# Attention, gated convolution and spatial gating on one core: block moves by DMA, convolution taps over batch borders, and another order in the first tile

## The chip, the cores and the metric

The kernel runs on one core of a Trainium2 chip. The metric is the device time of one execution in microseconds (us), median of several runs. TensorE (PE) has a clock gate with two levels, 1.2 and 2.4 GHz; the granted clock in the profile is the share of the full one.

## What is computed

Eight batches of 576 tokens. First an attention within chunks of 64 tokens (8 heads of 64), then a gated feed-forward layer with a convolution over three tokens, then a second layer with a spatial mix; all in float32. The change lies in the first two:

```
scores = scale * (q_c @ k_c.T)                    # per chunk of 64 tokens
scores = scores - max(scores)
attn = exp(scores) / (sum(exp(scores)) + 1e-9)
x = attn @ v_c
h = maximum(x @ w_in, 0)
conv = cw[0]*h[t-1] + cw[1]*h[t] + cw[2]*h[t+1]   # zero beyond a batch's first and last token
gate = 1 / (1 + exp(-conv))
y = (h * gate) @ w_out
```

The convolution doesn't cross from one batch into the next: the first token of a batch has no left neighbour, the last no right one. The 4608 tokens are laid in one row, so that a batch border falls inside a tile of tokens.

## The kernel before

Phase A makes attention and the first layer, phase B the second layer. Phase A goes over ten tiles (`TILES`: eight of 512 tokens, two of 256); a tile has `KF` = 8 slots, one for each 128 rows of `w_in`'s output. Slot s = 8 * tile + f. In each slot, `moe_in(s)` makes 12 matmuls into a PSUM tile `h` (three products of high and low halves, L467), `moe_h(s)` the ReLU (L487, ScalarE, ACT) and the convolution: the middle tap `c = h * cw[1]` (L492 on GpSimd, POOL, in slots below `START` = 9, else L494 on ACT), then the outer taps on VectorE (DVE, L500). A tap writes only columns that have their neighbour in the same batch, so where a border lies in a tile each outer tap is two instructions (`runs` gives the pieces), and a slot has four. `moe_tanh(s - 1)` (L509, ACT), `moe_g(s - 1)` (L513, DVE) and `moe_split(s - 2)` (high and low half, ACT L521 and DVE L79 `gl`) follow in later slots, and `moe_out` sums the slot into four PSUM tiles `acc` (L546): of slot s-2 for the first tile, of slot s-3 afterwards. The first tile's `moe_out` uses the float32 weights `w2f`, 8 matmul records per slot.

Attention goes in 18 groups of 256 tokens, two to a 512 tile, each in two halves j. `att_s` makes scores (L255, PE) in PSUM `a0`/`a1`; `att_sm1` takes the maximum (L270 `mx`) and the difference (L276 `e`) on DVE, `att_exp` the exponential on ACT (L299, one instruction), `att_sm2` sum (L310), inverse and product (L319) on DVE. For halves listed in `ACC`, the subtraction and the sum go with eight exponentials on ACT (L294). The block P must be transposed for P @ V: groups below `NP` = 6 do it by PE (`att_tp`, L358 `tp`) and an ACT copy (L364); the later groups by DVE's transpose of 32x32 pieces (L328 `t`), after which 8 blocks of 32 partitions move into `pt`: four that stay in their partitions by POOL copies (L339), four by DMAs of SP's queue (L341). `att_pv` (L397 `px`, L416 `x`) multiplies by V into PSUM `a0`/`a1` again, and its result goes to `xh`, `xl`.

`FIRST_SLOTS`, `S_SLOT` and `PV_SLOT` say in which slot a group's scores and products stand: from tile 4 on, a tile's first group has its scores in slot 5 of the tile two before and its product in slot 1 of the tile before, the second group scores in slot 3 and product in slot 7, of the tile before. Halves j = 0, 1 go through the softmax in the slot of the scores and the next one. `start_slot` writes out slots 0 to 8, the loop behind it the others; every engine does its instructions in the order in which this code issues them. A prelude ahead of slot 0 does groups 0 and 1.

Of the kernel before, what the change touches and what calls it, by code (L numbers as in the profile page):

```python
# [7 lines left out]
F32 = mybir.dt.float32  # L8
# [33 lines left out]
LAG0 = 2  # L42
# [2 lines left out]
P0 = sum(g[0] == 0 for g in GROUPS)  # L45
NP = 6

ACC = ((0, 1), (2, 0), (2, 1), (3, 0), (3, 1))
RBUFS = 4

S_SLOT = (-3, 3)
PV_SLOT = (1, 7)

FIRST_SLOTS = {1: ((1, 5), (4, 8)), 2: ((1, 5), (3, 8)), 3: ((-1, 3), (1, 7))}

LATE_S = ()

FRONT = (0, 7)
NS = KF * NT
START = KF + 1  # L60
WMAX = 64 * max(TILES)

# [9 lines left out]
def attention_moe_kernel(ctx: ExitStack, tc: tile.TileContext, qT, kT, vL, vP, eye, w1, cw, w2, w3, wsp, wsr, bsp, w4, out):  # L72
# [103 lines left out]
    def phase_a(mid):  # L176
# [124 lines left out]
        def sm2_steps(g, j):  # L301
# [23 lines left out]
            def turn():  # L325

                t = ap.tile([128, 2, 8, 32], F32, tag="t", name="t", bufs=2)
                nc.vector.transpose(  # L328
                    out=t[:, :, :nu, :].rearrange("p h u j -> p u h j"),
                    in_=e.rearrange("p u (h i) -> p u h i", h=2),  # L330
                )
                pt = d["pt", j] = ap.tile([128, 2, 8, 32], F32, tag="pt", name="pt", bufs=4)
                for hh in range(2):
                    for qh in range(2):
                        for kh in range(2):
                            s0, o0 = 64 * hh + 32 * qh, 64 * hh + 32 * kh
                            dst, src = pt[o0:o0 + 32, qh, :nu, :], t[s0:s0 + 32, kh, :nu, :]
                            if qh == kh:
                                nc.gpsimd.tensor_copy(out=dst, in_=src)  # L339
                            else:  # L340
                                nc.sync.dma_start(out=dst, in_=src)  # L341

            return ([] if acc else [total]) + [eps, inverse, norm]

# [94 lines left out]

            return high, low  # L440

        hs, hhs, gs, accs = {}, {}, {}, {}

        carry = mp.tile([128, KF, 2], F32, name="carry", bufs=1)

# [34 lines left out]
        def moe_h(s, between=lambda: None):  # L480
# [7 lines left out]
            if i < NT - 1:  # L488
                nc.gpsimd.tensor_copy(out=carry[:, f, :], in_=h[:, w + b - 2:])
            c = mp.tile([128, WMAX], F32, tag="c", name="c", bufs=3)[:, :n]  # L490
            if s < START:
                nc.gpsimd.tensor_scalar_mul(c, h[:, o:o + n], cws[:, 1, f:f + 1])  # L492
            else:
                nc.scalar.activation(out=c, in_=h[:, o:o + n], func=AF.Copy, scale=cws[:, 1, f:f + 1])  # L494
            prev = runs(n, lambda j: o + j > 0 and (t0 + j) % S != 0)
            nxt = runs(n, lambda j: o + j + 1 < w + b and (t0 + j) % S != S - 1)
            between()
            for tap, step, segs in ((0, -1, prev), (2, 1, nxt)):
                for a, z in segs:
                    nc.vector.scalar_tensor_tensor(  # L500
                        out=c[:, a:z], in0=h[:, o + a + step:o + z + step], scalar=cws[:, tap, f:f + 1],
                        in1=c[:, a:z], op0=ALU.mult, op1=ALU.add,
                    )
            gs[s] = (h[:, o:o + n], c)

        def moe_tanh(s):
            _, c = gs[s]

            nc.scalar.activation(out=c, in_=c, func=AF.Tanh, scale=0.5)  # L509

# [136 lines left out]
        def scores(s):  # L647
            if s in at:
# [4 lines left out]
                for j in range(2):  # L653
                    if s < START:
                        todo.setdefault((s, 1), []).append((g, j))
                        todo[s + 1, 2 + j] = [(g, j)]
                        todo[s + 2, 4] = [(g, 1)]
                        if g < NP:
                            todo[s + 2, 5 + j] = [(g, j)]
# [12 lines left out]

        def start_slot(s):

            moe_hh(s)
            tps = [att_tp(*h) for h in todo.pop((s, 5), [])]
            if s < KF:
                moe_in(s)
            if s == KF:
                xh, xl = values(s)  # L680
            scores(s)
            if s:
                moe_tanh(s - 1)
                moe_g(s - 1)
            for f in tps:
                f()
            att_sm2(*todo.pop((s, 4), []))
            tps = [att_tp(*h) for h in todo.pop((s, 6), [])]
            first.load(2)
            if s == 4:  # L690
                load_v(3)
            weave(first.merge(2))
            soft = todo.pop((s, 2), [])
            for h in soft:
                att_exp(*h)
            att_sm2(*soft)
            if s == KF:
                xh()
                xl()
            if s >= LAG0:  # L700
                moe_out(s - LAG0)
            if s == KF:
                moe_in(s)
            moe_h(s)
            for f in tps:
                f()
            for h in todo.pop((s, 3), []):
                att_exp(*h)
            if first.merged:
                first.high()  # L710
                first.low()
            first.scale(2)
            if s < KF:
                xh, xl = values(s)
                xh()
                xl()
            att_sm1(*todo.pop((s, 1), []))

        def out(s):
            if s - LAG0 < KF:  # L720
# [4 lines left out]
        for s in range(NS + LAG):  # L725
# [17 lines left out]
                moe_hh(s)  # L743
            xs = ()
            tp = todo.pop((s, 7), None)
            if tp:
                tp = att_tp(*tp)
            if s % KF in FRONT:
                xs = values(s)
# [5 lines left out]
                moe_split(s - 2)  # L755
            if s < NS + 1:
                moe_tanh(s - 1)
            if tp:
# [338 lines left out]
```

## Time and profile before

| | before |
|---|---|
| median of 3 runs | 953.56 us (953.29 to 954.04) |
| profiled execution, device time | 949.09 us |
| its span in the trace | 947.0 us |
| mean granted TensorE clock | 0.982 |
| busy: PE, DVE, ACT, POOL | 906.8, 597.8, 419.7, 146.5 us (96, 63, 44, 15% of the span) |

The profiled execution is one run; what lies around its span is 2.1 us, and it is 4.5 us below the median. Phase A takes the span's first 523 us, phase B the rest. A busy share is a mean over stages that differ; where PE stands still is to be read from the order of time.

### The profile page before, as it was taken

Reading aid. Unit: us, or ns where it says so; the run is one execution under the profiler, and the core shown is the slowest. Engines: PE = TensorE matmul, PEld = TensorE weight load, DVE = VectorE, ACT = ScalarE, POOL = GpSimd, SP = SyncE. Lnnn points to the kernel's source line nnn. Section 1 sums busy time; section 2 is a strip of 40 time slices with the busy share of each in tenths; the row PEclk is TensorE's granted clock in tenths of the full one; section 3 lists DMA queues with packets and bytes.
Section 4 is the critical chain, followed back from the end, with each engine's and each line's share of the span. In section 5 each row is a group of like instructions: output and inputs, shape, how many; then the busy total and the mean of one; then the engine's idle time right before and its main releaser. Section 6 shows DMA issues by size and latency. Waiting matters only on the chain.

```text
span 947.0 us, 17151 instructions
## 1 busy us (share of the span) xinstructions
PE 906.8 (96%) x6804; PEld 769.8 (81%) x6804; DVE 597.8 (63%) x1173; ACT 419.7 (44%) x869; POOL 146.5 (15%) x305
## 2 busy tenths in 40 slices
PE   7699788999999999999999999999999999999998
PEld 6465567877777787778899898989898898989897
DVE  5775787998979798885767575451717162542522
ACT  4554453555564544546467454242423333332321
POOL 0221233232413233230311020010001000000000
PEclk8889999999999999999999999999999999999999
DMA  9551223434242341321023431112020302020001
GB/s 302 186 183 46 90 67 102 144 103 140 88 131 84 96 145 34 120 83 46 12 83 87 145 115 51 46 45 84 1 84 13 116 13 82 13 67 12 22 24 56
DMA packets 62352, 79.52 MB, mean 84 GB/s; under 512 B 6720, under 2 KB 49856, under 8 KB 62144
## 3 DMA queue, kind: packets, MB, share of 16 engines
q1 hardware_dynamic: 62272, 78.43, 26.1%
q8 instruction: 53, 0.87, 0.4%
q14 instruction: 27, 0.22, 0.1%
HBM read 54.29 MB, written 18.87 MB: 77 GB/s over the span
## 4 chain that ended last, share of the span: by engine, by line
PE 77%; DVE 10%; issue 4%; ACT 3%; DMA 2%; POOL 2%; SPq 1%; ACTq 0%; POOLq 0%
PE h L467 15%; PE acc L546 14%; PE pss L971 13%; PE psu L937 11%; PE pso L990 11%; PE psv L885 10%; DVE c L500 3%; PE x L416 1%; POOL c L492 1%; DVE gl L79 1%; DMA x2d<-x 1%; DVE mx L270 1%; DVE e L276 1%; DVE e L319 1%; PE s L255 1%
## 5 line engine op out<-in xcount | busy, mean ns | idle before, releaser
L500 DVE SCALAR_TENSOR_TENSOR c<-hh,nr,c 128x257 f32<-128x257 f32 (+28 forms) x272 | 134.9, 546 | 62.6 <-ACT c L494 43.7
L973 DVE TENSOR_TENSOR gf<-pss,bb 128x288 f32<-128x288 f32 x64 | 28.9, 452 | 146.5 <-PE pss L971 146.5
L509 ACT ACTIVATE c<-c 128x512 f32<-128x512 f32 (+2 forms) x80 | 47.5, 594 | 109.1 <-DVE c L500 109.1
L467 PE MATMUL h<-xh,w1h 128*128 128x512 f32 (+1 forms) x320 | 89.1, 402 | 1.0 <-DVE xh L434 0.9
L467 PE MATMUL h<-xh,w1l 128*128 128x512 f32 (+1 forms) x320 | 83.8, 385 | 0.0
L467 PE MATMUL h<-xl,w1h 128*128 128x512 f32 (+1 forms) x320 | 81.2, 376 | 0.0
L971 PE MATMUL pss<-wsh,vl 128*128 128x288 f32 x256 | 75.4, 295 | 0.0
L971 PE MATMUL pss<-wsh,vh 128*128 128x288 f32 x256 | 75.4, 294 | 0.0
L971 PE MATMUL pss<-wsl,vh 128*128 128x288 f32 x256 | 75.3, 294 | 0.0
L546 PE MATMUL acc<-gh,w2l 128*128 128x512 f32 (+2 forms) x288 | 71.5, 370 | 0.0
L546 PE MATMUL acc<-gl,w2h 128*128 128x512 f32 (+2 forms) x288 | 71.4, 370 | 0.0
L546 PE MATMUL acc<-gh,w2h 128*128 128x512 f32 (+2 forms) x288 | 71.2, 369 | 0.0
L467 PEld LDWEIGHTS h<-xh,w1l 128*128 128x128 f32 x320 | 59.4, 196 | 13.1 <-DVE w1l L79 0.4
L975 ACT CAST gth<-gf 128x288 fp32r<-128x288 f32 x64 | 27.7, 433 | 95.5 <-DVE gf L974 95.5
L339 POOL COPY pt<-t 32x256 f32<-32x256 f32 x96 | 49.7, 518 | 126.2 <-issue 60.0
L467 PEld LDWEIGHTS h<-xl,w1h 128*128 128x128 f32 x320 | 57.8, 191 | 12.2
L467 PEld LDWEIGHTS h<-xh,w1h 128*128 128x128 f32 x320 | 56.7, 196 | 13.6 <-issue 1.4
L487 ACT ACTIVATE hh<-h 128x512 f32<-128x512 f32 (+1 forms) x80 | 44.0, 550 | 37.9 <-PE h L467 37.8
L983 POOL CAST grh<-gth 128x256 fp32r<-128x256 f32 x8 | 5.3, 668 | 358.0 <-ACT gth L975 358.0
L79 DVE TENSOR_TENSOR gl<-c,gh 128x512 fp32r<-128x512 f32 (+2 forms) x72 | 52.6, 730 | 11.6 <-ACT gh L521 11.6
L546 PEld LDWEIGHTS acc<-gh,w2l 128*128 128x128 f32 x288 | 50.8, 188 | 10.2
L546 PEld LDWEIGHTS acc<-gl,w2h 128*128 128x128 f32 x288 | 50.8, 188 | 10.2
(126 smaller groups left out, 1910.5 us busy)
## 6 DMA issues: line engine op xcount, KB each, us to landing
raw<-in_w_dram SPq DMA_DIRECT2D x26, 512.0 KB, 4.9
x2f<-x2d SPq DMA_DIRECT2D x32, 288.0 KB, 3.1
q<-in_qT_dram SPq DMA_DIRECT2D x16, 512.0 KB, 3.9
k<-in_kT_dram SPq DMA_DIRECT2D x16, 512.0 KB, 4.9
out_dram<-o SPq DMA_DIRECT2D x32, 256.0 KB, 2.1
v<-in_vP_dram SPq DMA_DIRECT2D x6, 512.0 KB, 6.1
v<-in_vL_dram SPq DMA_DIRECT2D x12, 256.0 KB, 3.6
v<-in_vL_dram SPq DMA_DIRECT2D x24, 128.0 KB, 3.5
```

The costliest lines, as they stand in the source:

```text
L79: eng.tensor_tensor(out=lo, in0=full, in1=hi, op=ALU.subtract)
L339: nc.gpsimd.tensor_copy(out=dst, in_=src)
L467: nc.tensor.matmul(ph, wt[:, k, f * 128:(f + 1) * 128], x[:, k, :w], start=n == 0, stop=n == 11)
L487: nc.scalar.activation(out=h[:, b:], in_=ph, func=AF.Relu)
L500: nc.vector.scalar_tensor_tensor(out=c[:, a:z], in0=h[:, o + a + step:o + z + step], scalar=cws[:, tap, f:f + 1], in1=c[:, a:z], op0=ALU.m ...
L509: nc.scalar.activation(out=c, in_=c, func=AF.Tanh, scale=0.5)
L546: nc.tensor.matmul(accs[m], w[:, f, m * 128:(m + 1) * 128], x, start=f == 0 and j == 0, stop=f == KF - 1 and j == len(terms) - 1,)
L885: nc.tensor.matmul(ps, x[:, k, sl], w[:, k, DV:], start=i == 0, stop=i == 11)
L937: nc.tensor.matmul(ps[:, :HB], w[:, k, d * 128:(d + 1) * 128], x[:, k, t], start=i == 0, stop=i == 11)
L971: nc.tensor.matmul(o, a[:, ds], w, start=i == 0, stop=i == len(mm) - 1)
L973: nc.vector.tensor_tensor(out=gf, in0=o, in1=bb[:, t], op=ALU.add)
L990: nc.tensor.matmul(ps, x[:, k, sl], w[:, k, :], start=i == 0, stop=i == 11)
```

## The change

1. All eight blocks of a transposed half move by DMA from SP's queue (96 POOL copies become 96 more DMAs).
2. Outer taps are one instruction each, over the batch border. The two columns at the border that so get a wrong neighbour are made again by ACT: a product `m` of the middle tap (one column), and, ahead of `moe_tanh`, an activation that adds the one right neighbour to it. That is four ACT instructions of one column in each of 56 slots, and two DVE instructions fewer.
3. `ACC` keeps only (0, 1): the halves of groups 2 and 3 take the difference and the sum on DVE and one exponential on ACT.
4. In slots below `START` the middle tap is on ACT, not on POOL.
5. Slots 0 to 7 get an order written as a list (`ORDER`); slot 8 keeps its own (`LAST_ORDER`). PE's transposes move behind `moe_out`. In later slots, `TP_LATE` puts the transposes behind `moe_in`. The scores of group 5 move from slot 13 to slot 12, and the copies `xh` behind the exponential.

```diff
-ACC = ((0, 1), (2, 0), (2, 1), (3, 0), (3, 1))
+ACC = ((0, 1),)
-FIRST_SLOTS = {1: ((1, 5), (4, 8)), 2: ((1, 5), (3, 8)), 3: ((-1, 3), (1, 7))}
+FIRST_SLOTS = {1: ((1, 5), (4, 8)), 2: ((1, 4), (3, 8)), 3: ((-1, 3), (1, 7))}
+ORDER = "hh in s g norm1 load merge exp0 norm0 out tp0 h pt0 exp1 split scale tp1 pt1 pv x max"
+LAST_ORDER = "hh tp0 pv s g pt0 norm1 tp1 load merge exp0 norm0 x out in h pt1 exp1 split scale max"
+TP_LATE = True
@@ turn
-                            if qh == kh:
-                                nc.gpsimd.tensor_copy(out=dst, in_=src)
-                            else:
-                                nc.sync.dma_start(out=dst, in_=src)
+                            nc.sync.dma_start(out=dst, in_=src)
@@ moe_h
-            if s < START:
-                nc.gpsimd.tensor_scalar_mul(c, h[:, o:o + n], cws[:, 1, f:f + 1])
-            else:
-                nc.scalar.activation(out=c, in_=h[:, o:o + n], func=AF.Copy, scale=cws[:, 1, f:f + 1])
+            nc.scalar.activation(out=c, in_=h[:, o:o + n], func=AF.Copy, scale=cws[:, 1, f:f + 1])
-            for tap, step, segs in ((0, -1, prev), (2, 1, nxt)):
+            fixes[s] = []
+            for tap, step, segs, other in ((0, -1, prev, nxt), (2, 1, nxt, prev)):
+                if len(segs) == 2:
+                    (a, j), (_, z) = segs
+                    segs = [(a, z)]
+                    m = mp.tile([128, 1], F32, tag="m", name="m", bufs=8)
+                    nc.scalar.activation(out=m, in_=h[:, o + j:o + j + 1], func=AF.Copy, scale=cws[:, 1, f:f + 1])
+                    fixes[s].append((c[:, j:j + 1], h[:, o + j - step:o + j - step + 1], cws[:, 2 - tap, f:f + 1], m))
@@ moe_tanh
+            for dst, src, w, m in fixes.pop(s):
+                nc.scalar.activation(out=dst, in_=src, func=AF.Identity, scale=w, bias=m)
@@ the loop over slots from START on
-            if tp:
+            if tp and not TP_LATE:
                 tp = att_tp(*tp)
...
-            if xs:
-                xs[0]()
             if soft:
                 att_sm1(soft)
                 att_exp(*soft)
+            if xs:
+                xs[0]()
...
                 moe_in(s)
+                if tp and TP_LATE:
+                    tp = att_tp(*tp)
                 moe_h(s)
+                if tp and TP_LATE:
+                    tp()
```

**PE, slots 2 and 3.** `h` rows are `moe_in`, `acc` rows `moe_out`, `tp` rows the transposes of group 2's two halves. Before, from the `moe_out` of slot 2 to that of slot 3:

```order
L546 MATMUL acc_575<-c,w2f 128x512
L358 MATMUL tp<-idt,e 128x128 x4
L467 MATMUL h<-xh,w1h 128x512 x4
L467 MATMUL h<-xl,w1h 128x512 x4
L467 MATMUL h<-xh,w1l 128x512 x4
L358 MATMUL tp<-idt,e 128x128 x4
L546 MATMUL acc_572<-c,w2f 128x512
```

And now:

```order
L555 MATMUL acc_569<-c,w2f 128x512
L468 MATMUL h<-xh,w1h 128x512 x4
L468 MATMUL h<-xl,w1h 128x512 x4
L468 MATMUL h<-xh,w1l 128x512 x4
L555 MATMUL acc_566<-c,w2f 128x512
L555 MATMUL acc_567<-c,w2f 128x512
L555 MATMUL acc_568<-c,w2f 128x512
L555 MATMUL acc_569<-c,w2f 128x512
L359 MATMUL tp<-idt,e 128x128 x8
```

Both transposes now stand behind the `moe_in` and `moe_out` of slot 3.

**DVE, slots 19 to 20.** From the transpose `t` of the half of slot 19 to the subtraction of the next half. Before:

```order
L328 STREAM_TRANSPOSE t<-e 128x8x2x32
L500 SCALAR_TENSOR_TENSOR c<-hh,nr,c 128x129
L500 SCALAR_TENSOR_TENSOR c<-hh,nr,c 128x382
L500 SCALAR_TENSOR_TENSOR c<-hh,nr,c 128x128
L500 SCALAR_TENSOR_TENSOR c<-hh,nr,c 128x383
L79 TENSOR_TENSOR gl<-c,gh 128x512
L270 TENSOR_REDUCE mx<-s 128x8
L276 TENSOR_TENSOR e<-s,mx 128x512
```

And now:

```order
L332 STREAM_TRANSPOSE t<-e 128x8x2x32
L507 SCALAR_TENSOR_TENSOR c<-hh,nr,c 128x512 x2
L83 TENSOR_TENSOR gl<-c,gh 128x512
L274 TENSOR_REDUCE mx<-s 128x8
L280 TENSOR_TENSOR e<-s,mx 128x512
```

Four taps have become two, and nothing else has moved there.

**SP's queue, slots 19 to 21.** The stores `x2d` of the tile before, the block moves of group 7, and the loads of `q` and `k`. Before:

```order
L530 DMA x2d_58<-x_1769 512x1x447
L341 DMA pt<-t 32x256 x8
L216 DMA q<-in_qT_dram 128x4x256
L216 DMA k<-in_kT_dram 128x4x256
```

And now:

```order
L539 DMA x2d_58<-x_1787 512x1x447
L342 DMA pt<-t 32x256 x16
L220 DMA q<-in_qT_dram 128x4x256
L220 DMA k<-in_kT_dram 128x4x256
```

The order of the queue is the same; two halves have 16 moves instead of 8.

## Rows read from the trace of the kernel before

**Rows 1.** The page: granted clock in 40 slices of the span, in tenths.

```profile
PEclk8889999999999999999999999999999999999999
```

**Rows 2.** Timeline of PE, 40 to 155 us: start, length, instructions, [idle before <-releaser].

```profile
46.31 1.09 PE L358 MATMUL tp<-idt,e 128*128 128x128 f32 x4 [6.46 <-DVE e L319]
47.05 2.06 PE L467 MATMUL h<-xh,w1h 128*128 128x512 f32 x4
...
52.31 0.60 PE L358 MATMUL tp<-idt,e 128*128 128x128 f32 x4
...
82.53 0.63 PE L358 MATMUL tp<-idt,e 128*128 128x128 f32 x4 [1.67 <-DVE e L319]
...
110.04 0.82 PE L358 MATMUL tp<-idt,e 128*128 128x128 f32 x4 [4.25 <-DVE e L319]
...
141.50 1.97 PE L255 MATMUL s<-k,q 64*64 64x64 f32 x60 [2.81 <-ACT pt L364]
...
152.69 1.16 PE L397 MATMUL px<-pt,v 64*64 64x64 f32 x62 [2.70 <-DVE e L276]
```

**Rows 3.** Chain that ended last, pieces with a whole `moe_in`: start, length.

```profile
110.86 4.17 PE h L467 x12
...
143.47 3.49 PE h L467 x12
...
252.57 2.99 PE h L467 x12
...
413.82 4.53 PE h L467 x12
```

**Rows 4.** Timeline of PE, products of the second group (two of five).

```profile
198.67 1.24 PE L416 MATMUL x<-pt,v 64*64 64x64 f32 x60 [1.44 <-DMA pt<-t]
...
412.59 1.24 PE L416 MATMUL x<-pt,v 64*64 64x64 f32 x60 [2.23 <-DMA pt<-t]
```

**Rows 5.** Timeline of DVE, slots 17 to 22.

```profile
165.89 1.67 DVE L500 SCALAR_TENSOR_TENSOR c<-hh,nr,c 128x129 f32<-128x129 f32 x4 [0.61 <-ACT c L494]
...
174.63 0.68 DVE L270 TENSOR_REDUCE mx<-s 128x8 f32<-128x512 f32 x1
...
186.75 2.12 DVE L500 SCALAR_TENSOR_TENSOR c<-hh,nr,c 128x129 f32<-128x129 f32 x4
...
197.07 0.68 DVE L270 TENSOR_REDUCE mx<-s 128x8 f32<-128x512 f32 x1
197.78 0.69 DVE L276 TENSOR_TENSOR e<-s,mx 128x512 f32<-128x512 f32 x1
```

**Rows 6.** Groups by line and shape, whole span: xcount | busy us, mean ns | idle.

```profile
L513 DVE SCALAR_TENSOR_TENSOR c<-c,hh 128x512 f32<-128x512 f32 x64 | 43.8, 685 | 5.2 <-ACT c L509 5.2
...
L494 ACT ACTIVATE c<-hh,nr 128x512 f32<-128x512 f32 x55 | 39.9, 725 | 6.6 <-POOL hh L477 2.0
...
L492 POOL TENSOR_SCALAR c<-hh,nr 128x512 f32<-128x512 f32 x9 | 16.2, 1801 | 0.1
...
L894 ACT ACTIVATE sd<-mv,epst 128x1 f32<-128x1 f32 x36 | 10.6, 295 | 38.3 <-DVE mv L892 38.3
```

**Rows 7.** Timeline of all engines, 41 to 49 us (slots 1 and 2).

```profile
41.34 0.66 ACT L90 ACTIVATE w2f<-raw 128x512 f32<-128x512 f32 x1 [2.40 <-DMA raw<-in_w_dram]
...
42.55 0.69 DVE L513 SCALAR_TENSOR_TENSOR c<-c,hh 128x512 f32<-128x512 f32 x1 [0.80 <-ACT c L509]
...
45.03 0.17 DVE L313 TENSOR_SCALAR sm<-sm 128x8 f32<-128x8 f32 x1
...
45.47 0.69 DVE L319 TENSOR_TENSOR e<-e,rs 128x512 f32<-128x512 f32 x1
...
47.63 1.54 DVE L500 SCALAR_TENSOR_TENSOR c<-hh,nr,c 128x511 f32<-128x511 f32 x2 [1.47 <-POOL c L492]
```

**Rows 8.** Timeline of SP's queue, the second half of group 7.

```profile
186.85 2.41 SPq L341 DMA_DIRECT2D pt<-t  x4
```

**Rows 9.** The page, DMA issues: xcount, KB each, median us to landing.

```profile
pt<-t SPq DMA_DIRECT2D x96, 32.0 KB, 1.9
```

More of the change, by code (lines that the diff above doesn't have):

```diff
@@ L440, in att_pv @@
             return high, low
-        hs, hhs, gs, accs = {}, {}, {}, {}
+        hs, hhs, gs, accs, fixes = {}, {}, {}, {}, {}
         carry = mp.tile([128, KF, 2], F32, name="carry", bufs=1)
@@ L497, in moe_h @@
             between()
-            for tap, step, segs in ((0, -1, prev), (2, 1, nxt)):
+            fixes[s] = []
[6 more added lines that the diff above has]
+                    fixes[s].append((c[:, j:j + 1], h[:, o + j - step:o + j - step + 1], cws[:, 2 - tap, f:f + 1], m))
+                    assert any(a <= j < z for a, z in other)
                 for a, z in segs:
@@ L656, in scores @@
                         todo[s + 1, 2 + j] = [(g, j)]
+                        todo[s + 1, 8] = [(g, 0)]
                         todo[s + 2, 4] = [(g, 1)]
@@ L673, in start_slot @@
         def start_slot(s):
[L675 to L717, printed above, removed]
+            pend = {}
+            def transposes(k):
+                pend[k] = [att_tp(*h) for h in todo.pop((s, k), [])]
+            def product():
+                pend["x"] = values(s)
+            def high_low():
+                if first.merged:
+                    first.high()
+                    first.low()
@@ new lines, in exps, with call, tanh_g, loads @@
+            def exps(k):
+                for h in todo.pop((s, k), []):
+                    att_exp(*h)
+            def call(k):
+                for f in pend.pop(k):
+                    f()
+            def tanh_g():
+                if s:
+                    moe_tanh(s - 1)
+                    moe_g(s - 1)
+            def loads():
+                first.load(2)
+                if s == 4:
+                    load_v(3)
+            steps = {
+                "hh": lambda: moe_hh(s),
+                "tp0": lambda: transposes(5),
+                "pt0": lambda: call(5),
+                "tp1": lambda: transposes(6),
+                "pt1": lambda: call(6),
+                "in": lambda: moe_in(s),
+                "s": lambda: scores(s),
+                "max": lambda: att_sm1(*todo.pop((s, 1), [])),
+                "exp0": lambda: exps(2),
+                "exp1": lambda: exps(3),
+                "norm0": lambda: att_sm2(*todo.pop((s, 8), [])),
+                "norm1": lambda: att_sm2(*todo.pop((s, 4), [])),
+                "g": tanh_g,
+                "load": loads,
+                "merge": lambda: weave(first.merge(2)),
+                "split": high_low,
+                "scale": lambda: first.scale(2),
+                "out": lambda: moe_out(s - LAG0) if s >= LAG0 else None,
+                "h": lambda: moe_h(s),
+                "hmax": lambda: moe_h(s, steps["max"]),
+                "pv": product,
+                "x": lambda: call("x"),
+            }
@@ L719, in out @@
+            for k in (ORDER if s < KF else LAST_ORDER).split():
+                steps[k]()
         def out(s):
@@ L757, in phase_a @@
                 moe_tanh(s - 1)
-            if tp:
+            if tp and not TP_LATE:
                 tp()
-            if xs:
-                xs[0]()
             if soft:
```

## The prediction, before the run

> **What bounds the kernel now.** The busy shares come first: PE is busy 96% of the span, so whatever is to be gained are PE's gaps and the stretches in which its clock is low. The granted clock is full in nearly every slice from the fourth on, and low in the first three [rows 1]. The second view is PE's timeline in phase A: where does it stand idle, and who ends the wait? In phase B and after 415 us it shows no wait worth counting; the change reaches neither. Before 26 us stands the prelude, whose instructions the change leaves alone. So all is decided between 26 and 415 us, in two kinds of waits.
>
> The first kind stands in tiles 0 and 1. PE waits 6.46 us at 46.31 for group 2's softmax product, 1.67 at 82.53 and 4.25 at 110.04 for the same product of later halves, 2.81 at 141.50 for the ACT copy that frees the score PSUM, and 2.70 at 152.69 for the subtraction of group 6, whose scores occupy the PSUM that `px` needs [rows 2]. Together 17.9 us. Waits also cost clock. A whole `moe_in` takes 2.99 us at 2.4 GHz; the first after the 6.46 us runs from 47.05 to 52.31, its first four matmuls in 2.06 us [rows 2], and the ones after 110.86 and 143.47 take 4.17 and 3.49 [rows 3]. That adds 2.3 + 1.2 + 0.5 = 4.0. First kind: 21.9 us.
>
> The second kind comes once in a tile, ahead of the second group's product (slots 23, 31, 39, 47, 55): 1.44 us the first, 2.23 the last [rows 4], the three between 2.1 each, 9.9 in all. The view names a DMA `pt<-t`; I read it otherwise. The move of that half was issued at 186.85 [rows 8], ten microseconds earlier. What ends at 198.47, 0.2 us before PE goes on, is DVE's subtraction of the next group's second half [rows 4, 5]: it frees the PSUM bank `a1`. So it is DVE's pace that holds PE: `mx` at 174.63 and 197.07 are three slots apart, 7.48 us each [rows 5], while PE would need 5.6 to 6.7 (two blocks of 12 matmuls, every second slot the scores too). The `moe_in` behind the first two of these waits is at full clock (252.57: 2.99 us), behind the last at 4.53 [rows 3]; three are like the last, so 4.4 us of clock. Second kind: 14.3 us.
>
> **Steady slots: two taps instead of four.** The four pieces take 2.12 us beside POOL's copies, and 1.67 when POOL is still [rows 5]; two instructions of 512 columns take at most 2 x 0.685 = 1.37 [rows 6]. With the copies gone, a softmax slot is 0.75 us shorter in its taps, and a little more in `gl`, which also lay beside the copies: I take 0.8, so 6.67 us. From `mx` of slot 19 at 174.63 [rows 5], three slots later is 194.64, and the subtraction ends 1.40 later (as 197.07 to 198.47 [rows 5]), at 196.04. PE would arrive at 198.67 - 1.44 = 197.23 [rows 4]. The wait goes, with 1.2 us to spare; at the worst place 3 x 0.8 = 2.4 stands against 2.23, just enough. I count all 14.3.
>
> **What ACT pays.** Four one-column instructions per slot. The nearest row is the one-column square root with a pointer bias, 295 ns [rows 6]. Two stand ahead of tanh: 0.6 us between the end of the taps and tanh. The cover: DVE first does `gl`, `mx` and the subtraction, about 2 us, before it wants tanh for `moe_g`; 0.6 + 0.64 fits. Bounds: nothing (the two overlap with the end of the one before), or 0.6 per slot if that cover is gone, which would eat three quarters of the 0.8.
>
> **What SP pays.** A block of four moves takes 2.41 us to issue [rows 8], of eight 4.8; the last lands 1.9 later [rows 9]. For slot 23 the half's transpose ends at 186.85, so the last piece lands at 186.85 + 4.8 - 0.6 + 1.9 = 193.0 against PE's 197.2: hidden, by 4.2 us. Behind these moves in the queue stand loads that are needed a slot or more later. Tightest is slot 17: the transpose ends some 5.5 us after `px` starts (`xl` and the rest of the softmax lie between), moves and landing add 6.1, so 11.6; PE comes after 1.1 + four blocks of 2.8 = 12.3. I charge 0.5, bounds 0 and 2.5.
>
> **The first tile, laid out by hand.** The middle tap on ACT costs 0.73 instead of POOL's 1.80 [rows 6], so slot 0's taps and slot 1's maxima come 1.5 to 1.8 us earlier. That helps little: ACT still waits for a weight block that lands at 41.34, and tanh and the first exponential stand behind it, so `moe_g` starts at 42.55 as before [rows 7]. From there on, by the rows' own spacing: the merge up to 45.03, the sum 0.7 (an instruction of 512 columns, new), inverse and product 1.13 (45.03 to 46.16): the first half is done at 46.9; then taps 1.5, `w1l` 0.6, `moe_g` after tanh 0.7, the second half's 0.7 + 1.13: 51.55 [rows 6, 7]. On PE the old wait is gone: `moe_in(3)` from 39.86 to 42.9, 0.3 us for `moe_g`, `moe_out(1)` to 46.85, the first transpose; then 4.0 us for the second half at 51.55. Where the 6.46 wait was, two of 4.3 us now stand.
>
> The later ones by the same laying out: with the transposes behind `moe_out(5)`, the 1.67 becomes some 0.7 (ACT's copy ahead of `px`). At 110 us the chain from the four `x` copies over `gh`, `gl`, `mx`, exponential and product is unchanged, but PE has 3 us more work before it: 4.25 becomes 1.9. The 2.81 disappears, since group 5 is done a slot earlier and its copies are out of the PSUM before slot 15. The 2.70 stays as 2.4: DVE is 0.8 faster there, and PE comes earlier too. Sum of waits 0.3 + 4.0 + 0.7 + 1.9 + 2.4 = 9.3 instead of 17.9.
>
> Their clock: 6.46 and 4.25 us were followed by slow matmuls, 2.70 and 1.44 not [rows 2, 3]. I charge 1.5 for the wait of 4 us and 0.5 for the others. The Trainium skill (TensorE: Matmul & The Clock Gate, Part 1: The HAM clock gate) says that the gate follows how busy PE has lately been and falls to half after idling, wherever the wait comes from. By that, each of the three waits could be charged 1.5, 4.5 in all, and the gain would be 21.8 instead of 24.3; the rows here show it for some waits of 2 us and not for others. First kind after: 9.3 + 2.0 = 11.3, a gain of 10.6.
>
> **Sum.** 10.6 + 14.3 - 0.5 = 24.4 us, against the profiled execution's own 949.09: 924.7. The median lies 4.5 us above that execution, so I forecast 953.56 - 24.4, about 929 us.
>
> **Rivals.**
> 1. DVE's slot shortens less than 0.8 us, because the corrections push tanh and with it the exponential and the sum. For it: the margin at the worst place is 0.2 us. Against: 1.2 us at slot 23, and ACT is busy 44% of the span. Half of the second kind would stay, 7.2 us: 936. The Trainium skill (ScalarE: Activation LUTs, What ACT_TABLE_LOAD costs) prices every one-column pointer operand at about 93 ns; the correction has two, the square root's row one. By that page the pair would take some 0.75 us instead of 0.6, which is still covered; no row here shows such an instruction.
> 2. The first tile gains nothing: DVE has 2 x 0.69 more per half (subtraction and sum), and slots 1 to 3 hang on its chain. For it: 4 us of wait reappear two slots later. It decides when the second half ends after 58 us instead of 51.55. Price 10.6: 940.
> 3. Slower: a block of eight outlasts its slack. Place: the twelve products from slot 17 on, for which SP moves 16 blocks per group. It decides when a block lands 4.2 us later than I work out, by eight moves that queue up on the same partitions. If each of the twelve then waited 2.5 us, 30 against 24.4: 959. Against: the median landing is 1.9 us [rows 9], and it would have to be over 6.
> 4. More gain: the wait at 51.55 shrinks by 2.5 and loses its clock, slot 16's wait goes: 6.4 more, 922.
>
> **How the numbers follow.** Forecast with its own range 924 to 933: 0.55; rival 1: 0.16; rival 2: 0.12; rival 4: 0.10; rival 3: 0.03; an outcome within 0.2% (1.9 us, about what a measurement can tell), where rivals 1 and 2 come together with a bad slot 17: 0.04. The range for 8 in 10 takes in rivals 1 and 4 and most of rival 2: 921 to 940. Faster 0.93, same 0.04, slower 0.03.
>
> **What would show it.** Right: no wait ahead of the `x` products in slots 23, 31, 39, 47, 55, `mx` rows 6.5 to 6.7 us apart, a PE wait near 47 to 51 us for group 2's second half, none at slot 15, one of 2 to 3 us at slot 16's `px`. Wrong: waits for `pt<-t` that end with a DMA landing; `mx` rows still over 7 us apart; tanh late; a span before 155 us that has not shrunk by about 10.

## The result, and the profile after

The changed kernel takes 927.62 us (median of 4 runs, 925.71 to 928.94) against 953.42 us before on the same chip: ratio 0.9733, 95% interval 0.9707 to 0.9759. A second set of runs gave 926.86 against 949.90: 0.9757, 0.9727 to 0.9787. The forecast was about 929 in 921 to 940. In microseconds of the medians the two sets say 25.8 and 23.0; the forecast gain was 24.4. The profiled execution after has 928.94 us and a span of 927.2, which is 19.8 less than the 947.0 before; that of the second set has 927.38 and 925.6.

From the page of the changed kernel, busy times, the chain by engine, two groups (xcount | busy us, mean ns | idle before) and the block moves:

```profile
PE 903.1 (97%) x6804; PEld 768.4 (83%) x6804; DVE 579.4 (62%) x1065; ACT 475.5 (51%) x1042; POOL 74.5 (8%) x200
...
PE 92%; DVE 3%; ACT 2%; DMA 1%; issue 1%; SPq 0%; ACTq 0%
...
L516 ACT ACTIVATE c<-hh,m,nr 128x1 f32<-128x1 f32 x112 | 37.5, 384 | 55.8 <-DVE c L507 55.8
L522 DVE SCALAR_TENSOR_TENSOR c<-c,hh 128x512 f32<-128x512 f32 (+2 forms) x80 | 50.7, 633 | 21.9 <-ACT c L518 21.2
...
pt<-t SPq DMA_DIRECT2D x192, 32.0 KB, 1.8
```

PE alone is now 92% of the chain. PE's busy time fell by 3.7 us with the same matmuls, which I read as clock; the other 16 us of the span are waits. The moves land as quickly as before (1.8 us) though there are twice as many.

Timeline of PE of the changed kernel, 40 to 155 us, which answers to [rows 2]:

```profile
52.81 1.08 PE L359 MATMUL tp<-idt,e 128*128 128x128 f32 x4 [4.03 <-DVE e L323]
53.54 2.05 PE L468 MATMUL h<-xh,w1h 128*128 128x512 f32 x4
...
107.61 0.63 PE L359 MATMUL tp<-idt,e 128*128 128x128 f32 x4 [1.58 <-DVE e L323]
112.53 1.15 PE L398 MATMUL px<-pt,v 64*64 64x64 f32 x62 [1.24 <-ACT pt L365]
115.09 0.33 PE L259 MATMUL s<-k,q 64*64 64x64 f32 x4 [1.41 <-DVE xl L83]
115.69 1.76 PE L259 MATMUL s<-k,q 64*64 64x64 f32 x60 [0.26 <-DVE xl L83]
...
146.71 1.98 PE L398 MATMUL px<-pt,v 64*64 64x64 f32 x62 [3.36 <-DVE e L280]
```

With 0.24 and 0.16 at 84 us these waits sum to 12.3 us, against 17.9 before (18.9 with 0.74 at 102 and 0.22 at 138 us, which the prediction left out) and a forecast of 9.3. The 6.46 us and the 2.81 us are gone and the 4.0 us stands where it was laid out. New are the two at 112 and 115 us.

The chain of the changed kernel, start and length, pieces with low clock, which answer to [rows 3]:

```profile
53.89 4.70 PE h L468 x12
...
117.45 3.90 PE h L468 x12
...
148.69 3.67 PE acc L555 x12
```

Against 2.99 for a `moe_in` and 2.80 for a `moe_out` at full clock that is 1.7 + 0.9 + 0.9 lost; the slow scores (1.76 instead of 1.16) and the slow `px` (1.98) add 1.4, so 4.9 in all. The prediction put the kernel before at 4.0, without the slow scores at 141.50 (1.97 instead of 1.16); counted in the same way, with them, it lost 4.8.

One loss in this trace is not the change's. Slot 0's first matmuls run at a granted clock of 0.50 in this execution, and at 1.00 in that of the second set, though the kernel is the same. First execution of the changed kernel:

```profile
26.07 2.04 PE L468 MATMUL h<-xh,w1h 128*128 128x512 f32 x4 [0.92 <-DVE xh L435]
...
33.91 1.16 PE L259 MATMUL s<-k,q 64*64 64x64 f32 x64
...
503.14 1.09 PE L913 MATMUL psv<-w3h,x2h 128*128 128x512 f32 x4
```

The one of the second set:

```profile
25.84 1.17 PE L468 MATMUL h<-xh,w1h 128*128 128x512 f32 x4 [0.93 <-DVE xh L435]
...
31.96 1.16 PE L259 MATMUL s<-k,q 64*64 64x64 f32 x64
...
145.07 1.16 PE L398 MATMUL px<-pt,v 64*64 64x64 f32 x62 [3.37 <-DVE e L280]
```

And the kernel before, with the two ends of the stretches measured further below:

```profile
31.98 1.16 PE L255 MATMUL s<-k,q 64*64 64x64 f32 x64
...
410.02 0.33 PE L416 MATMUL x<-pt,v 64*64 64x64 f32 x4
...
523.04 1.09 PE L885 MATMUL psv<-w3h,x2h 128*128 128x512 f32 x4
```

From slot 0's first matmul to slot 1's scores that is 7.84 us against 6.12 and 6.10. Six of this case's fourteen profiled executions have the loss. It is passed on: in all three traces the weight block for which ACT, and `moe_g` behind it, wait at 41 to 42 us is issued on SP's queue 2.55 to 2.56 us after slot 1's scores start. So the first tile is measured from these scores on (31.98, 33.91 and 31.96 us) to the end of slot 16's `px`, and the later slots from there to phase B's first matmul.

Timeline of DVE, softmax slots of tile 2, which answers to [rows 5]:

```profile
174.84 1.50 DVE L507 SCALAR_TENSOR_TENSOR c<-hh,nr,c 128x512 f32<-128x512 f32 x2
176.85 0.69 DVE L274 TENSOR_REDUCE mx<-s 128x8 f32<-128x512 f32 x1
...
183.53 0.69 DVE L274 TENSOR_REDUCE mx<-s 128x8 f32<-128x512 f32 x1
...
190.18 0.68 DVE L274 TENSOR_REDUCE mx<-s 128x8 f32<-128x512 f32 x1
```

The maxima are 6.66 us apart, 7.48 before. The second group's products on PE, answering to [rows 4]:

```profile
192.49 1.16 PE L417 MATMUL x<-pt,v 64*64 64x64 f32 x64
...
242.30 1.80 PE L417 MATMUL x<-pt,v 64*64 64x64 f32 x64
```

The first of the five has no gap. In the other four (1.80, 1.81, 1.80, 1.80) the 64 matmuls take 0.64 us longer than 1.16: a gap after the first four, too short for the view to name. The clock behind them stays full.

### The profile page after: what moved, and what is told of

It reads as the page before. It is cut to its first block, busy times and chain, and to the rows that moved or that the text cites. A ratio compares the mean times of both kernels' runs of the same rounds, so it can differ in the third digit from the quotient of the medians.

```text
span 927.2 us, 17210 instructions
## 1 busy us (share of the span) xinstructions
PE 903.1 (97%) x6804; PEld 768.4 (83%) x6804; DVE 579.4 (62%) x1065; ACT 475.5 (51%) x1042; POOL 74.5 (8%) x200
## 4 chain that ended last, share of the span: by engine, by line
PE 92%; DVE 3%; ACT 2%; DMA 1%; issue 1%; SPq 0%; ACTq 0%
PE h L468 21%; PE acc L555 20%; PE pss L999 13%; PE psu L965 11%; PE pso L1018 11%; PE psv L913 11%; PE s L259 2%; PE x L417 2%; PE px L398 1%; DVE c L507 1%; DMA raw<-in_w_dram 1%; DMA k<-in_kT_dram 1%; SPq L220 0%; DVE e L323 0%; DVE gl L83 0%
## 5 line engine op out<-in xcount | busy, mean ns | idle before, releaser
L507 DVE SCALAR_TENSOR_TENSOR c<-hh,nr,c 128x512 f32<-128x512 f32 (+3 forms) x160 | 115.0, 719 | 48.3 <-ACT c L492 45.0
L468 PE MATMUL h<-xh,w1l 128*128 128x512 f32 (+1 forms) x320 | 81.4, 376 | 0.0
L468 PEld LDWEIGHTS h<-xh,w1l 128*128 128x128 f32 x320 | 57.8, 191 | 12.2
L468 PEld LDWEIGHTS h<-xl,w1h 128*128 128x128 f32 x320 | 57.7, 191 | 12.2
L516 ACT ACTIVATE c<-hh,m,nr 128x1 f32<-128x1 f32 x112 | 37.5, 384 | 55.8 <-DVE c L507 55.8
L522 DVE SCALAR_TENSOR_TENSOR c<-c,hh 128x512 f32<-128x512 f32 (+2 forms) x80 | 50.7, 633 | 21.9 <-ACT c L518 21.2
L83 DVE TENSOR_TENSOR gl<-c,gh 128x512 fp32r<-128x512 f32 (+2 forms) x72 | 54.3, 754 | 12.2 <-ACT gh L530 12.1
L555 PEld LDWEIGHTS acc<-gh,w2h 128*128 128x128 f32 x288 | 50.8, 190 | 9.5
```

Of the source, the lines that this page charges most:

```text
L83: eng.tensor_tensor(out=lo, in0=full, in1=hi, op=ALU.subtract)
L468: nc.tensor.matmul(ph, wt[:, k, f * 128:(f + 1) * 128], x[:, k, :w], start=n == 0, stop=n == 11)
L507: nc.vector.scalar_tensor_tensor(out=c[:, a:z], in0=h[:, o + a + step:o + z + step], scalar=cws[:, tap, f:f + 1], in1=c[:, a:z], op0=ALU.m ...
L516: nc.scalar.activation(out=dst, in_=src, func=AF.Identity, scale=w, bias=m)
L522: nc.vector.scalar_tensor_tensor(out=c, in0=c, scalar=1.0, in1=h, op0=ALU.add, op1=ALU.mult)
L555: nc.tensor.matmul(accs[m], w[:, f, m * 128:(m + 1) * 128], x, start=f == 0 and j == 0, stop=f == KF - 1 and j == len(terms) - 1,)
```

## The experiments

Each was timed in five rounds beside the kernel before on its chip. The ratios below are to that, with the 95% interval.

### The later slots alone

```diff
-ACC = ((0, 1),)
+ACC = ((0, 1), (2, 0), (2, 1), (3, 0), (3, 1))
-FIRST_SLOTS = {1: ((1, 5), (4, 8)), 2: ((1, 4), (3, 8)), 3: ((-1, 3), (1, 7))}
+FIRST_SLOTS = {1: ((1, 5), (4, 8)), 2: ((1, 5), (3, 8)), 3: ((-1, 3), (1, 7))}
-TP_LATE = True
+TP_LATE = False
...
+            if s < START:
+                nc.gpsimd.tensor_scalar_mul(c, h[:, o:o + n], cws[:, 1, f:f + 1])
+            else:
```

and the former `ORDER` (diff further below) and place of the copies `xh`. With `TP_LATE = False` the later order of the transposes is gone too, though the text below counts it in: what this kernel keeps of the change are its parts 1 and 2, the block moves and the taps.

> The later slots' parts alone: DMA moves for all blocks, one tap instruction over the border with the corrections on ACT, and the later order of the transposes; the first tile (middle tap on POOL, exponentials by eights for groups 2 and 3, order, scores of group 5 in slot 13) is as before. My theory: this part is worth 14.3 us by the forecast, 14.6 by the traces of before and after, so about 14 to 15 us under before, ratio 0.985. The waits ahead of the products of slots 23, 31, 39, 47 and 55 are under 0.5 us, maxima of one softmax slot to the next 6.66 us; before 155 us the waits of before are back (6.5 at 46 us, 1.7, 4.2, 2.8, 2.7). Rival: the first tile's gain is what lets the later slots run without waits (PE and DVE come there with another lead), then waits of 1 us or more stay in those slots and the gain is under 10 us (ratio over 0.990).

Measured: 936.30 us against 950.30, ratio 0.9856 (0.9833 to 0.9879), a gain of 14.0 us (11.5 to 15.9 by the interval), where 14 to 15 was expected. Its PE timeline has the first tile's waits of before again, and none in the later slots:

```profile
45.35 1.09 PE L359 MATMUL tp<-idt,e 128*128 128x128 f32 x4 [6.17 <-DVE e L323]
...
140.40 1.97 PE L259 MATMUL s<-k,q 64*64 64x64 f32 x60 [3.25 <-ACT pt L365]
153.08 1.98 PE L398 MATMUL px<-pt,v 64*64 64x64 f32 x62 [3.12 <-DVE e L280]
```

The late slots need no help from the first tile. The rival falls.

### The first tile alone

```diff
+                            if qh == kh:
+                                nc.gpsimd.tensor_copy(out=dst, in_=src)
+                            else:
                                 nc.sync.dma_start(out=dst, in_=src)
...
-                if len(segs) == 2:
+                if False and len(segs) == 2:
```

> The first tile's parts and the new order alone: four of eight blocks are copied by POOL again, and the taps are split at the border, without corrections, as before. My theory: what is left is the first kind. By the forecast it is worth 10.6 us (ratio 0.989), by the traces of before and after only 5 to 7 (0.993 to 0.995): the trace is to be believed, so 5 to 8 us under before. The waits ahead of the products of slots 23 to 55 are back with 1.4 to 2.4 us each and slow matmuls behind three of them. Rival: the new order in the later slots (transposes behind the matmuls of the slot, copies of x behind the exponential) is what removes the second kind; then those waits stay away and this kernel is within 5 us of the changed one.

Measured: 941.24 against 950.30, ratio 0.9908 (0.9887 to 0.9929), a gain of 9.1 us; the interval reaches from 6.7 to 10.7, so the expected 5 to 8 was too low by the median and is not excluded. On PE the second kind of waits is back:

```profile
193.38 1.24 PE L420 MATMUL x<-pt,v 64*64 64x64 f32 x60 [1.43 <-DMA pt<-t]
...
246.02 1.24 PE L420 MATMUL x<-pt,v 64*64 64x64 f32 x60 [2.08 <-DMA pt<-t]
```

Order and late transposes do nothing for them. 14.0 + 9.1 = 23.1: the two parts add up to the whole (23.0 in the second set, 25.8 in the first). The traces say the same: the first kernel's later slots take 13.5 us less than before (355.7 instead of 369.2), the second kernel's first tile 7.6 less (114.3 instead of 121.9); together 21.1, where the changed kernel's two traces gain 21.8 and 21.4 from slot 1's scores to phase B.

### Four taps, and POOL's copies: which half of the later slots' part

The first kernel takes the second hunk of the diff above alone, the second the first hunk alone.

> The changed kernel with the outer taps split at the border again (four instructions a slot, no corrections on ACT); all blocks still move by DMA. My theory of the DVE slot: it has shortened by 0.4 us from fewer tap instructions and 0.4 from POOL being still, so here the maxima are 6.9 to 7.1 us apart (7.48 before, 6.66 after), the products of slots 23 to 55 wait 0 to 0.6 us and the time is 1 to 3 us above the changed kernel, ratio to before 0.974 to 0.977. Rival A (only the number of tap instructions counts): maxima 7.3 to 7.5 apart, waits of 1.4 us and more, 8 to 14 us above the changed kernel. Rival B (corrections on ACT cost more than the merged taps give back): as fast as the changed kernel or faster.

> The changed kernel with four of a half's eight blocks copied by POOL again and four moved by DMA, as before; the taps stay one instruction each. My theory: two taps beside POOL's copies take 1.7 to 2.0 us instead of 1.4 to 1.5, gl a little more, the maxima are 7.0 to 7.2 us apart, the products of slots 23 to 55 wait 0.5 to 1.2 us each, and the time is 4 to 9 us above the changed kernel, ratio to before 0.977 to 0.983. Rival A (a quiet POOL is all that counts): maxima 7.4 to 7.5 apart, 10 to 14 us above. Rival B (only the number of tap instructions counts): maxima 6.7 apart and the time of the changed kernel, ratio 0.973.

Measured: 928.81, ratio 0.9775 (0.9752 to 0.9798), and 928.64, ratio 0.9781 (0.9757 to 0.9805). By the medians each is 1.8 to 2.0 us above the changed kernel's second set, which ran on another chip; the intervals overlap with those of both its sets (the first, up to 0.9759, only just), so the times alone don't show a difference. The 4 to 9 us expected of the second kernel did not come. DVE with four taps and a still POOL:

```profile
180.27 1.63 DVE L507 SCALAR_TENSOR_TENSOR c<-hh,nr,c 128x129 f32<-128x129 f32 x4
...
182.43 0.68 DVE L274 TENSOR_REDUCE mx<-s 128x8 f32<-128x512 f32 x1
...
189.21 0.68 DVE L274 TENSOR_REDUCE mx<-s 128x8 f32<-128x512 f32 x1
```

and DVE and POOL with two taps beside the copies:

```profile
178.53 1.51 DVE L510 SCALAR_TENSOR_TENSOR c<-hh,nr,c 128x512 f32<-128x512 f32 x2
178.74 2.80 POOL L343 COPY pt<-t 32x256 f32<-32x256 f32 x4 [3.70 <-DVE t L332]
179.97 0.88 DVE L83 TENSOR_TENSOR gl<-c,gh 128x512 fp32r<-128x512 f32 x1
```

The maxima are 6.78 to 6.81 us apart in the first, 6.86 to 6.87 in the second, 6.66 in the changed kernel and 7.48 before. My theory had the two halves add (0.4 + 0.4) and gave 6.9 to 7.2. They don't: either alone saves 0.6 to 0.7 of the 0.82. Four short taps lose 0.49 us beside the copies (2.12 in [rows 5] against 1.63 here); two long ones lose nothing there (1.51 against 1.50), POOL loses instead (2.80 for its four copies, 2.18 before), and only `gl` grows by 0.2. The Trainium skill (SBUF — State Buffer, SBUF: two separate sides) says that VectorE and GpSimd share one port pair, which whoever starts first holds for a whole instruction, for a VectorE instruction with two SBUF inputs against one of GpSimd that reads SBUF. The trace agrees in that POOL's copies stretch beside the taps. It does not show why four taps are held up and two are not: DVE starts 0.2 us ahead of the copies in both kernels (186.75 against 186.96 before, 178.53 against 178.74 here).

The price of either half can be read from the products: they take 0.64 us more than 1.16 each in the changed kernel, 2.19 - 1.16 = 1.03 with four taps (240.90 to 243.09) and 2.37 - 1.16 = 1.21 with POOL's copies (239.16 to 241.53). That makes 4 x 0.39 = 1.6 and 4 x 0.57 = 2.3 us more, in line with the medians.

### The changed kernel again, as a yardstick

> The changed kernel, unaltered, beside the three others on the same chip, since two runs of a kernel on different chips differ by 1 to 3 us and the next effects are as small. My theory (the two halves of the change add up: 14.0 of the later slots and 9.1 of the first tile, as measured apart): ratio to before 0.974 to 0.977. Rival (the first run's 0.9733 is this kernel's true ratio and the two parts help one another): 0.971 to 0.974.

Measured: 926.86 (926.29 to 927.38), ratio 0.9757, inside the theory's bounds; the rival's 0.971 to 0.974 lies within the interval too, so this doesn't exclude it.

### Corrections issued twice

```diff
+                for _ in range(2):
-                nc.scalar.activation(out=dst, in_=src, func=AF.Identity, scale=w, bias=m)
+                    nc.scalar.activation(out=dst, in_=src, func=AF.Identity, scale=w, bias=m)
```

> Each correction of a border column is issued twice with the same operands and result, so two more one-column instructions stand ahead of tanh in 56 slots. My theory: they take 0.66 us per pair, tanh comes 0.7 us later, ACT's wait of 0.54 us ahead of the exponential goes and the exponential comes 0.1 to 0.2 us later per softmax slot: maxima 6.7 to 6.9 us apart instead of 6.66, waits ahead of the products of slots 23 to 55 up to 0.8 instead of 0.4, the time 0 to 2 us above the changed kernel. Rival 1 of the prediction (the cover is used up): maxima 7.3 apart, waits of 1.5 us and more, 6 to 10 us above the changed kernel.

Measured: 939.99 against 949.90, ratio 0.9898 (0.9869 to 0.9927), 13.1 us above the changed kernel on the same chip. The theory's step was right (maxima 6.67, 6.93, 6.92 apart, ACT's wait ahead of the exponential gone) and its price, 0 to 2 us, far too low. From the timeline of this kernel, ACT in a softmax slot, DVE in a slot without one, and PE:

```profile
175.55 1.51 ACT L517 ACTIVATE c<-hh,m,nr 128x1 f32<-128x1 f32 x4 [1.99 <-DVE c L507]
...
210.52 0.69 DVE L523 SCALAR_TENSOR_TENSOR c<-c,hh 128x512 f32<-128x512 f32 x1 [1.69 <-ACT c L519]
...
230.47 1.15 PE L259 MATMUL s<-k,q 64*64 64x64 f32 x60 [1.26 <-DVE e L280]
...
244.26 1.34 PE L417 MATMUL x<-pt,v 64*64 64x64 f32 x60 [1.02 <-issue]
```

The cover that I had worked out (`gl`, maximum, subtraction) exists in softmax slots only. In the four slots of a tile without a softmax DVE waits for tanh: up to 0.16 us before, up to 0.86 in the changed kernel, mostly 0.6 to 2.0 here (and 0.36 in most softmax slots); over the span 5.5, 21.2 and 49.1 us. In the changed kernel PE does not wait for it. Here DVE enters the softmax slots late: the first maximum starts 4.65 us after the tile's scores end (217.59 to 222.24) instead of 2.67 (216.90 to 219.57). From there on each tile is longer: three of them take 159.1 us from first maximum to first maximum (169.30 to 328.39) instead of 152.0 (168.55 to 320.53), 7.1 of the 10.4 us by which the two profiled spans differ.

### Moves issued twice

```diff
+                            for _ in range(2):
-                            nc.sync.dma_start(out=dst, in_=src)
+                                nc.sync.dma_start(out=dst, in_=src)
```

> Every block move is issued twice with the same result, so a half has 16 moves on SP's queue. My theory: each move costs SP 0.6 us of issue, so the last lands 4.8 us later; at slot 23 the slack of 4.2 to 4.5 us is used up (wait 0 to 1 us), at slots 17 to 22 products wait up to 5 us for a landing, 12 products in all lie in reach, and the queue's other entries come later too: 5 to 25 us above the changed kernel, and the waits ahead of the products now end with the landing of pt. Rival (the slack is larger than worked out, or the moves' engines take them side by side): under 3 us above the changed kernel and no wait of over 0.5 us ahead of a product. Rival 3 of the prediction (moves that queue up on the same partitions): more than 25 us above.

Measured: 1242.80 against 951.41, ratio 1.3068 (1.3038 to 1.3099). My theory's 25 us and the first rival are far off; the other rival's "more than 25" takes the time in, but for another reason. SP's queue in this kernel, and PE's waits of the whole span (us, times, longest):

```profile
162.49 20.30 SPq L343 DMA_DIRECT2D pt<-t  x16
```

```profile
PE x L418 <- DMA pt<-t: 277.4, 35, 12.4
```

against the two halves, 16 moves, of the changed kernel:

```profile
174.94 11.61 SPq L342 DMA_DIRECT2D pt<-t  x16
```

The experiment did more than it should: the second move of a pair writes the same place as the first, and the program makes SP wait until that has landed (196 semaphore instructions at this line instead of 24; 192 waits for `pt<-t`, 260 us in all, the longest 5.1), so a move costs 1.27 us instead of 0.6, and a half 20.3 us. It is no test of a doubled issue time. Nor is all of the time waits: the mean granted clock of this execution is 0.875 instead of 0.987. What it shows is that SP's queue decides when a half takes 20.3 us and one should come every 6.66: PE waits 35 times for a landing ahead of a product. In the changed kernel eight moves take 5.0 to 5.8 us of the 6.66. Where between 5.8 and 20.3 the waits set in wasn't tried.

### Three parts of the first tile, each undone alone

The old `ACC` and POOL's middle tap in slots below `START` are edits of the first experiment; the old order is

```diff
-ORDER = "hh in s g norm1 load merge exp0 norm0 out tp0 h pt0 exp1 split scale tp1 pt1 pv x max"
+ORDER = "hh tp0 in s g pt0 norm1 tp1 load merge exp0 norm0 out h pt1 exp1 split scale pv x max"
```

> The changed kernel with the exponentials of groups 2 and 3 by eights on ACT again, with their sums there. My theory: DVE is spared 2 x 0.69 us per half but ACT takes over 1 us more per half behind tanh, so the wait for group 2's second half (4.0 us at 52 us) changes by under 1.5 us in either direction: within 2 us of the changed kernel. Rival 2 of the prediction (DVE's subtraction and sum are what holds the first tile): the wait falls to under 2.5 us and the time by 2 to 4 us.

> The changed kernel with the former order of the first tile's slots (transposes ahead of the matmuls of a slot), everything else as changed. My theory: this order is what carries the first tile's gain; with it, group 2's first half is waited for ahead of slot 3's matmuls (3.5 to 6 us at 45 us) and the second half a slot later, together 5 to 8 us, and the time is 3 to 7 us above the changed kernel. Rival: the order is worth nothing by itself, and the middle tap on ACT or the scores of group 5 a slot earlier carry the gain: within 1.5 us.

> The changed kernel with the middle tap of slots 0 to 8 on POOL again, at 1.80 us instead of 0.73. My theory: at the start little changes, since the first gate waits for ACT's weight block, but the taps of slots 2 to 8 end 1.1 us later, and DVE's chain for group 2's second half with them: the wait at 52 us grows by 0.5 to 1.5 us, the time by 0 to 3 us. Rival A: no effect at all (within 0.5 us), the middle tap is hidden wholly. Rival B: it is what carries the first tile's gain, 5 us or more above the changed kernel.

Measured, beside 951.41: 927.07, ratio 0.9739 (0.9716 to 0.9762); 929.86, 0.9772 (0.9751 to 0.9793); 926.83, 0.9736 (0.9715 to 0.9757). The changed kernel itself did not run in this set. By the medians the old order is 2.8 to 3.0 us above the two others and 3.0 above the changed kernel on the other chip, though the intervals overlap; by the traces its first tile takes 116.5 us instead of 114.3 to 114.8. So the order is worth some 2 to 3 us by itself, and the other two nothing that these runs can tell. Its PE timeline:

```profile
47.47 1.09 PE L359 MATMUL tp<-idt,e 128*128 128x128 f32 x4 [6.75 <-DVE e L323]
```

With the old `ACC` the wait for the second half is 5.11 instead of 4.03 us, so the difference and the sum on DVE, with one exponential, end that half 1 us earlier; my theory had left the sign open. With POOL's middle tap the wait at 52 us stays at 4.04, where I had expected 0.5 to 1.5 more; a wait at 108 us grows from 1.58 to 2.62 and the 1.24 behind it goes. Neither shows in the time. All undone together, with the scores of group 5 in slot 13 again and the later transposes early, cost some 9 us (936.30 in the first experiment, against 926.86 on another chip). The waits that only come back there are 4.57 us at 109 and 3.25 at 140. By the prediction's laying out the first belongs to the late transposes (PE has a `moe_in` less to do before it) and the second to the move of the scores. Neither was undone alone, so some 6 of these 9 us are not assigned by a run.

### A later transpose, and another PSUM for group 5

```diff
-                            todo[s + 2, 5 + j] = [(g, j)]
+                            todo[s + 2 + (g == 2 and j == 1), 5 + j] = [(g, j)]
...
-            for k in (ORDER if s < KF else LAST_ORDER).split():
+            for k in (ORDER4 if s == 4 else ORDER if s < KF else LAST_ORDER).split():
...
+ORDER4 = "hh in s g norm1 load merge exp0 norm0 out tp1 pt1 h exp1 split scale pv x max"
```

The second kernel has besides:

```diff
-                if g == 0:
+                if g in (0, 5):
                     px = [ps_h
```

> The changed kernel with the transpose of group 2's second half moved from slot 3 to slot 4 (still ahead of its product, which stands in slot 4; only slot 4 has an order of its own for it). My theory: the wait of 4.0 us at 52 us is DVE's chain for that half, with PE's transposes put too early; PE has the matmuls of slot 4 to do meanwhile, so the wait goes, and the slow matmuls behind it (1.7 us) too; 0.5 to 1 us comes back ahead of the product, and 0 to 2 us at slot 16, where PE now comes earlier to the subtraction that it waits for. In all 3 to 5 us under the changed kernel. Rival: DVE is the bound of the first tile, and what PE gains at 52 us it gives back in the later waits at 82 to 145 us (their sum grows by over 3 us): within 1.5 us of the changed kernel.

> As the late transpose of group 2, and the product px of group 5 besides goes to the PSUM of the next matmul group instead of the scores' PSUM, so that in slot 16 it does not stand behind the subtraction of group 6's scores. My theory: both waits go, the one at 52 us and the one of 3.4 us at 146 us with 0.8 to 1.0 us of slow matmuls behind it, while the bank it borrows makes the next matmuls of the slot wait for under 1 us: 5 to 8 us under the changed kernel, ratio to before 0.966 to 0.971. Rival: the wait at slot 16 only moves (the borrowed bank is freed by the copy of x, which stands behind the exponential on its engine): no better than the late transpose alone.

Measured: 923.02 (920.22 to 924.40), ratio 0.9715 (0.9687 to 0.9744), and 921.11 (920.53 to 922.60), ratio 0.9698 (0.9668 to 0.9728): 3.8 and 5.8 us under the changed kernel on the same chip, whose runs lie at 926.29 to 927.38. Both beat both kernels. Between the two the ranges overlap, so that the second edit adds anything rests on the traces: from slot 1's scores to phase B they take 466.1 and 463.4 us, the changed kernel 469.2 and 469.6. PE of the second one:

```profile
56.83 1.16 PE L399 MATMUL px<-pt,v 64*64 64x64 f32 x62 [1.54 <-ACT pt L366]
...
144.71 1.17 PE L469 MATMUL h<-xh,w1h 128*128 128x512 f32 x4 [1.41 <-DVE xl L84]
...
154.22 1.11 PE L418 MATMUL x<-pt,v 64*64 64x64 f32 x58 [0.62 <-DMA pt<-t]
```

The 4.03 us became 1.54 + 0.65 + 0.27 (for `xl`, at 61 us) without slow matmuls, the 3.36 us became 1.41 + 0.62. The last is slot 17: PE now comes there earlier and waits for its block to land.

## Why the prediction was right, step by step

**The second kind of waits** was DVE's pace and not the DMA that the view named. Slot 6.67 forecast, 6.66 measured; taps and POOL's silence together save 0.82, forecast 0.8. The stretch from the end of slot 16's `px` to phase B's first matmul took 369.2 us before (153.85 to 523.04), in the changed kernel 354.5 (148.69 to 503.14) and in the second set 355.4: 14.7 and 13.8 gained. The later slots alone gained 14.0. Forecast 14.3 less 0.5 for slot 17. That the size came out is partly luck. "All to go" was too much: 4 x 0.64 = 2.6 stayed, as the step that compared 2.4 with 2.23 left no room; slot 17 cost nothing. On the other side the 9.9 us of waits were too few: taken from the first of its 64 matmuls to the last (410.02 to 413.83 for the fifth), the five products before took 12.2 us more than 1.16 each. Two errors of some 2.5 us cancelled.

**The first tile** was mis-sized: 9.1 us by the medians (6.7 to 10.7), 7.1 and 7.6 by the two traces from slot 1's scores to the end of slot 16's `px` (121.9 us before, 114.8 and 114.3), where 10.6 was forecast; the text had named a stretch before 155 us that shrinks by less than about 10 as a sign against it, and that sign appeared. The waits fell by 5.6 us instead of 8.6, and the clock gave nothing back (4.8 before, 4.9 after) where 2.0 was forecast. Four things went wrong in the laying out. The scores of group 5, put a slot earlier, stand right behind the `px` of slot 11 and wait 1.41 + 0.26 for `xl` to free their PSUM; that `px` itself waits 1.24 for ACT's copy, which stands behind ReLU, middle tap and border products. Slot 16's wait was 3.36 instead of 2.4, since the two taps ahead of it take 2.38 us beside a POOL subtraction. And the clock took 4.9 instead of 2.0: the prediction had worked out 4.5 as well, with each of three waits charged alike, and set it aside; the trace is near that. The timeline of DVE and POOL at slot 16:

```profile
142.25 2.38 DVE L507 SCALAR_TENSOR_TENSOR c<-hh,nr,c 128x512 f32<-128x512 f32 x2
142.71 1.37 POOL L83 TENSOR_TENSOR w2l<-w2f,w2h 128x512 fp32r<-128x512 f32 x1 [1.09 <-ACT w2h L150]
```

I made POOL silent in the sum by taking its copies away, and forgot that it still makes the low halves of weights. The kernel with two taps and POOL's copies confirms it: there the subtraction stands behind the copies, the taps take 1.51 us and the wait is 2.69.

```profile
139.76 1.51 DVE L510 SCALAR_TENSOR_TENSOR c<-hh,nr,c 128x512 f32<-128x512 f32 x2
```

```profile
143.54 1.48 PE L401 MATMUL px<-pt,v 64*64 64x64 f32 x62 [2.69 <-DVE e L280]
```

Right were the 4.0 us at 52, the 2.81 gone, and that the middle tap on ACT helps little.

**The sum.** That 927.62 lies 1.4 us from 929 is closer than its parts deserve. The forecast gain of 24.4 was read from one execution; by spans the profiled executions give 19.8 and 21.4, by medians the two sets 25.8 and 23.0. The step that the prediction added from the profiled execution to the median (4.5 us up) did not hold for the changed kernel, whose medians lie 1.3 and 0.5 us below its profiled executions.

**The rivals.** The first (tanh pushed) did not happen, but its margin was misread: I looked for the cover in softmax slots and found 2 us; the price shows in the others, where there is none, and a second pair costs 13 us. The correction pair took 0.67 us (0.6 forecast), a single one 384 ns. The prediction's 0.75 is two instructions at the price of the Trainium skill (ScalarE: Activation LUTs, What ACT_TABLE_LOAD costs); the same section says that two in a row overlap by about 93 ns, so the estimate by that page should have been 0.65, which the trace bears out. The second rival is refuted by the gain of the first tile alone. For the third, SP issues the last block for slot 23 by 186.55 (the 16 moves above), so with 1.8 us it lands 4.1 us ahead of the product at 192.49: the 4.2 as worked out. Only in the last experiment, where PE comes earlier, does a product wait for a landing (0.62 us at slot 17). The fourth named the two waits that the last experiment then took away or shortened, by other edits: 5.8 us under the changed kernel, where 6.4 was given.

## What to carry to other kernels

When an engine that feeds PE is short by a little per slot, find the smallest cut that brings its slot under PE's pace: here either of two edits would have done nearly all, and the second bought some 2 us. Look for the cover of a new instruction in every kind of slot, not only in the busiest, and ask of each queue what share of the slot its entries take: a second pair of ScalarE's corrections already decides, and SP's moves take up to 5.8 us of 6.66. When work is brought forward, write down what stands right ahead of it on its engine and which buffer that still holds.

## What the runs showed of the hardware that was not expected

POOL's copies lengthen four taps of 128 to 383 columns by 0.49 us and two of 512 columns not at all, while a subtraction of 512 columns with two operands on POOL lengthens those two by 0.88 (2.38 against 1.50). The same matmuls of slot 0 ran at a granted clock of 0.50 in one execution and 1.00 in another of the same kernel. Two waits of equal length in the kernel before (2.09 us at 251.33, 2.08 at 303.98) are followed by a `moe_in` of 2.99 and one of 4.35 us.
